# An attention and FFN block with adaptive layer norm: attention stage through the list scheduler, x1 of two blocks turned on VectorE

## The chip, the cores and the metric

One core of a Trainium2 chip runs the whole kernel. Its engines work side by side, each through its own list of instructions in order: TensorE (PE; its weight loads are listed as PEld), VectorE (DVE), ScalarE (ACT), GpSimd (POOL) and SyncE (SP). POOL and SP also issue most of the DMA transfers, so that an issue stands in their list behind what came before it. The metric is the device time of one execution, in microseconds (us). Smaller is better.

## The reference

A block with modulated layer norms: linear attention with a residual, then dense, Mish, dense with a residual. S is 2048 rows, D is 512, F is 1792, and there are 32 heads of 16.

```python
mod = (silu(c) @ w_mod).reshape(1, 6, 1, 512)
sa, ca, ga, sb, cb, gb = (mod[:, i] for i in range(6))
h = layernorm(x) * (1 + ca) + sa
q, k, v = split_heads(h @ wqkv)
phi = lambda t: where(t > 0, t + 1, exp(t)) + 1e-6
pq, pk = phi(q), phi(k)
kv = einsum("bhsd,bhse->bhde", pk, v)
z = pk.sum(over s)
o = (pq @ kv) / (pq . z + 1e-6)
x1 = x + ga * (merge_heads(o) @ wo)
h = layernorm(x1) * (1 + cb) + sb
out = x1 + gb * (mish(h @ w1 + b1) @ w2)
```

## The kernel before

**Data.** The 2048 rows are four blocks of 512 (b = 0 to 3), each of four row tiles of 128 (t). Features lie in four chunks of 128 (g, j or k). A product in full precision is three float32r matmuls, of the upper and lower halves of its operands (hi x hi, lo x hi, hi x lo). A *split* makes these halves: ACT rounds to the upper (name ending in h), VectorE subtracts to get the lower (ending in l).

**First part** (to line 940): layer norm, k = phi(...) of all rows, and the sums that stand for kv and z. z_unit (435) multiplies the summed pk (tile ku) by ones in plain float32, so that each partition has all of z. bcast_row (537) turns four columns of the modulation tile mc into a row with a TensorE transpose and an ACT copy, stores the row to DRAM and loads it back to all partitions; it serves ga (for wo) and gb (for the second residual).

**Attention stage** (943 to 1162). This code is written in the order in which its instructions stand. `tick` runs the generators that `spawn` has put in a list, one step of each, after each product. q of blocks 0 and 1 comes out of a seven-product scheme (q_sevens, 492), q of blocks 2 and 3 from plain products (q_unit, 442). attend (943) makes the denominators of a block: 16 plain float32 matmuls for four chunks and row tiles (line 948), TINY and reciprocal on VectorE (952), a store of the 64 KB to DRAM (955), four loads that spread them to 128 partitions (959, tile rd), and q times rd on VectorE (967) with a split. kv_ps (1098) is the kv product, m_k is kv times wo, and o_unit (993) is one row tile of the attention's output: four chunks of three matmuls. o_post adds x to get x1 and stores that to the output in DRAM.

x1 is then normalised row by row (norm_first, norm_each), and the FFN needs it transposed, features on partitions. For blocks 0 and 1, transpose_f (1032) and tp_op (1870) do this on TensorE: four 128x128 transposes into one PSUM tile tp_n for each of four chunks, which ACT scales and shifts to hf_n. For blocks 2 and 3, norm_job (1788) stores the rows to a DRAM tile nd, squares_job (1809) loads them back in four strips of 32x32 squares (tile y_n), and turn_job (1818) transposes the squares on VectorE, after which ACT scales.

**FFN stage** (from 1163). It works on pairs of blocks (0 with 1, then 2 with 3) and on seven groups g of 256 hidden features, again with seven products in place of eight: pair gives the first dense layer (products A to G, of six matmuls each), unit the second (m1 to m7). Their operands are sums and differences of quarters: t1 to t4 of the transposed x1 (columns_job, 1830), s of w1 (rows_job), t of w2 (sums_job; sums_first, 818, for two groups that are made in the attention stage). A list scheduler sets the order: drive (1290) takes the next TensorE operation that can start by its own clocks, and beside it the *jobs*, generators of steps for the other engines. best_job (1225) picks, on the engine that can start earliest, the waiting step with the nearest due time. The due times and the durations assumed are the table T (27). What is emitted stands in the engines' lists in that order; the chip doesn't reorder it.

Of the kernel before, what the change touches and what calls it, by code (L numbers as in the profile page):

```python
# [13 lines left out]
P = 128  # L14
# [15 lines left out]
 'urgent': 2.8,  # L30
 'store_later': 10.8,
 'row_lead': 21.6,
 'columns': 94.0,
# [4 lines left out]
 'lead_r': 12,  # L38
 'sum_lead': 3,
 'row_0': 31.7,  # L40
 'row_step': 12.1,
 'blocks': 11.6,
 'blocks_early': 19.3,
 'out_due': 57.7,
 'out_at': 20.3,
 'early_due': 98.6,
 'early_at': -0.5,
 'norm_due': 60.2,
 'norm_at': 18.7,
# [5 lines left out]
 'mm': 0.2166,  # L55
 'slow': 1.06,
 'late': 0.596,
 'pool_issue': 1.099,
 'left_early': 17.4,
 'right_due': 0.3,  # L60
 'right_early': 14.3,
 'sum_due': 0.3,
 'sum_early': 19.5,
 'pace_a': 5.2,
 'pace_l': 3.5,
 'pair_l': 13.2,
 'seq_0': 'ABCD.E.FG',
 'seq_l': 'AB.CD.E.FG..',
 'copy_due': 12.9,
# [7 lines left out]
 'first': 2,  # L77
 'turn_late': [5.0, 2.0],
 'left_out': 10.0,
 'add': 2.8}  # L80

@with_exitstack
def block_kernel(ctx: ExitStack, tc: tile.TileContext, x, wqkv, wo, w1, b1t, w2, c, wmodt, out):
# [351 lines left out]
    def z_unit():  # L435

        u = ku.pop((0, 0))
        p = ps("h", "z")
        pe.matmul(p, ones, u, start=True, stop=True)
        act.activation(zbc, p, AF.Identity, bias=ztiny[:, 0:1])  # L440

    def q_unit(b, g):
        p = ps("h", f"pq_{b}_{g}")
        gs = slice(P * g, P * (g + 1))
        for k in range(4):
            mm3(p, [w[:, gs] for w in wq[k]], hT["x", b, k], k == 0, k == 3)
        pq[b, g] = sb(f"q_{b}_{g}")
        spawn(phi(p, f"q_{b}_{g}", pq[b, g]))

# [42 lines left out]
    def q_sevens(side):  # L492

        pa, pc, u1, u2, u3 = {}, {}, {}, {}, {}

        def result(b, g, p, u):
            if u is not None:
                c = sb(f"cq_{b}_{g}")
                dve.tensor_tensor(c, p, u, op=ALU.add)
                p = c  # L500
            pq[b, g] = sb(f"q_{b}_{g}")
            spawn(phi(p, f"q_{b}_{g}", pq[b, g], 0 if u is None else 1 + (b == 0)))

        def copy(p, name):
            u = sb(name)
            act.activation(u, p, AF.Copy)
            return u

        for o in range(2):
            pa[o] = q_product(o, "a11", "b11", "h")  # L510
            u1[o] = copy(pa[o], f"qu1_{o}")
        side(0)
        for o in range(2):
            p = q_product(o, "a12", "b21", ("h", "tp")[o])
            result(0, o, p, u1[o])
            q_product(o, "s2", "t2", onto=pa[o])
            u2[o] = copy(pa[o], f"qu2_{o}")
            side(1 + o)
        for o in range(2):
            q_product(o, "s3", "t3", onto=pa[o])  # L520
            u3[o] = copy(pa[o], f"qu3_{o}")
# [1527 lines left out]
```

## Time and profile before

| | |
|---|---|
| median of 3 runs | 477.7 us (477.52 to 477.88) |
| span of the profiled execution | 475.7 us |
| TensorE's last matmul ends at | 471.3 us |
| attention stage after the first part, roughly | 103 to 197 us |
| first product of the FFN (p_a) | 196.85 us |

The span is that of one execution under the hardware profiler, from the first instruction to the last; the runs' times are the device's and hold 2.0 us more. In the timeline's rows, start and duration are followed by engine, line, operation, output and inputs. Matmuls are pipelined, so that a record of 0.39 us reaches into the next: the pace is read from start to start. In rows of groups, the number behind the bar is busy time and mean, then the idle time ahead and who ended it.

### The profile page before, as it was taken

How to read it: one execution, taken by the hardware profiler on the slowest of the kernel's cores; microseconds unless marked ns; L12 is line 12 of the kernel's file. 1: busy time of each engine (PE TensorE's matmuls, PEld its weight loads, DVE VectorE, ACT ScalarE, POOL GpSimd, SP SyncE). 2: the span in 40 equal slices, each digit the busy share in tenths (PEclk: the TensorE clock that was granted, in tenths of full speed). 3: DMA queues.
4: the chain of work that ended last, by engine and by line, in shares of the span. 5: the costliest groups of instructions: out<-in, count | busy, mean ns of one | idle time of the engine just before them, and what ended most of it. 6: DMA issues, size and time to landing. Idle time of an engine off the chain costs nothing.

```text
span 475.7 us, 7248 instructions
## 1 busy us (share of the span) xinstructions
PE 468.3 (98%) x2292; PEld 385.0 (81%) x2292; DVE 419.8 (88%) x816; ACT 325.1 (68%) x593; POOL 150.6 (32%) x220
## 2 busy tenths in 40 slices
PE   8999999999999999999999999999999999999996
PEld 6788888878877888888788888888888887788886
DVE  6989989898999998998998999989875767999984
ACT  6776777866835988769979898576466657546330
POOL 4684331100022422214433130522131325607340
PEclk9999999999999999999999999999999999999999
DMA  8998599434888486339899451983352469999977
GB/s 301 400 357 225 159 192 280 128 106 136 289 227 246 148 261 230 119 126 320 223 318 314 168 162 59 206 275 122 104 156 67 116 196 234 240 319 184 261 113 132
DMA packets 80480, 97.76 MB, mean 206 GB/s; under 512 B 29521, under 2 KB 53081, under 8 KB 80442
## 3 DMA queue, kind: packets, MB, share of 16 engines
q1 hardware_dynamic: 54376, 57.82, 39.3%
q0 software_dynamic: 22752, 38.43, 32.8%
q10 hardware_dynamic: 3314, 1.05, 1.1%
q8 instruction: 18, 0.29, 0.3%
q14 instruction: 20, 0.16, 0.1%
HBM read 69.22 MB, written 31.99 MB: 213 GB/s over the span
## 4 chain that ended last, share of the span: by engine, by line
PE 93%; DVE 3%; issue 1%; DMA 1%; ACT 1%; POOL 0%; ACTq 0%; DVEq 0%
PE p_a L1567 20%; PE pa L1652 12%; PE p_s L1567 8%; PE pc L1652 5%; PE pb L1652 4%; PE pd L1652 4%; PE o L142 3%; PE o L144 3%; PE o L143 3%; PE pq_a L488 3%; PE gacc L144 2%; PE pk L144 2%; PE gacc L142 2%; PE pk L142 2%; PE gacc L143 2%; PE pk L143 2%
## 5 line engine op out<-in xcount | busy, mean ns | idle before, releaser
L1526 POOL DMA_DIRECT2D wt_m<-w2t x32 | 28.0, 1109 | 56.0 <-PE p_a L1567 13.4
L1582 ACT ACTIVATE u<-p_a 128x512 f32<-128x512 f32 x42 | 25.0, 596 | 30.3 <-PE p_a L1567 29.7
L1591 ACT ACTIVATE u_a<-c_a,b1c 128x512 f32<-128x512 f32 x42 | 30.2, 719 | 14.9 <-DVE c_a L1588 12.9
L1717 POOL DMA_DIRECT2D out_dram<-turned x20 | 23.3, 1727 | 35.9 <-DVE turned L1705 25.0
L1588 DVE TENSOR_TENSOR c_a<-p_s,u 128x512 f32<-128x512 f32 x28 | 19.3, 689 | 15.7 <-PE p_s L1567 8.2
L1541 DVE TENSOR_TENSOR u_a<-u_a,u_a 128x512 f32<-128x512 f32 x28 | 18.6, 683 | 0.0
L984 POOL DMA_DIRECT2D out_dram<-r x16 | 9.0, 562 | 26.2 <-DVE r L988 13.6
L278 POOL TENSOR_TENSOR rs_n<-rs_n,half 128x1 f32<-128x1 f32 x16 | 10.8, 676 | 19.6 <-DVE rs_n L304 10.0
L1526 POOL DMA_DIRECT2D wt_m<-w2d x13 | 12.8, 1228 | 10.4 <-DVE c_a L1588 5.0
L371 ACT ACTIVATE e_k<-pk 128x512 f32<-128x512 f32 x15 | 8.9, 591 | 10.5 <-PE pk L144 10.4
L955 POOL DMA_DIRECT2D rden_d<-rden x2 | 1.4, 721 | 44.9 <-DVE rden L953 44.9
L1588 DVE TENSOR_TENSOR c_a<-p_a,u 128x512 f32<-128x512 f32 x14 | 9.6, 688 | 4.4 <-PE p_a L1567 1.7
L1683 ACT ACTIVATE U<-pa,mc 128x512 f32<-128x512 f32 x10 | 6.9, 685 | 9.4 <-PE pa L1652 9.3
L374 DVE SCALAR_TENSOR_TENSOR ku<-e_k,relu_k 128x512 f32<-128x512 f32 x15 | 10.7, 714 | 2.8 <-ACT relu_k L372 2.6
L278 POOL TENSOR_TENSOR rs_x<-rs_x,half 128x1 f32<-128x1 f32 (+1 forms) x10 | 7.9, 792 | 16.0 <-DVE rs_x L273 14.6
L1619 ACT ACTIVATE u_a<-p_a,b1c 128x512 f32<-128x512 f32 x14 | 9.6, 686 | 4.4 <-PE p_a L1567 4.3
L1368 POOL DMA_DIRECT2D w1p<-w1d x13 | 9.9, 765 | 8.0 <-PE p_a L1567 3.5
L967 DVE SCALAR_TENSOR_TENSOR q<-q,rd 128x512 f32<-128x512 f32 x16 | 10.5, 686 | 1.5 <-DMA rd<-rden_d 1.5
L374 DVE SCALAR_TENSOR_TENSOR q<-e_q,relu_q 128x512 f32<-128x512 f32 x16 | 10.6, 686 | 0.3 <-ACT relu_q L372 0.3
L254 DVE SCALAR_TENSOR_TENSOR wm<-wm,sc_row 128x512 f32<-128x512 f32 x16 | 10.6, 680 | 0.0
L1344 ACT ACTIVATE l_m_0h<-u_a 128x512 fp32r<-128x512 f32 x12 | 7.5, 623 | 4.3 <-DVE u_a L1541 4.3
L1350 DVE TENSOR_TENSOR l_m_1l<-u_a,l_m_1h 128x512 fp32r<-128x512 f32 x12 | 8.2, 685 | 2.0 <-ACT l_m_1h L1344 2.0
(1446 smaller groups left out, 1877.2 us busy)
## 6 DMA issues: line engine op xcount, KB each, us to landing
wt_m<-w2t POOLq DMA_DIRECT2D x32, 256.0 KB, 4.2
wt_m<-w2t SPq DMA_DIRECT2D x22, 256.0 KB
r<-in_x_dram SPq DMA_DIRECT2D x16, 256.0 KB
out_dram<-r POOLq DMA_DIRECT2D x16, 256.0 KB, 3.7
x<-in_x_dram SPq DMA_DIRECT2D x15, 256.0 KB
wt_m<-w2d SPq DMA_DIRECT2D x15, 256.0 KB
w1d<-in_w_dram SPq DMA_DIRECT2D x4, 896.0 KB
w1p<-w1d SPq DMA_DIRECT2D x13, 256.0 KB
```

What stands on the lines that cost most here:

```text
L142: pe.matmul(o, st[0], mv[0], start=start, stop=False)
L143: pe.matmul(o, st[0], mv[1], start=False, stop=False)
L144: pe.matmul(o, st[1], mv[0], start=False, stop=stop)
L278: pool.tensor_tensor(y, y, half[:, lo:hi], op=ALU.pow)
L374: dve.scalar_tensor_tensor(dst, e, 1.0, r, op0=ALU.min, op1=ALU.add)
L1526: q.dma_start(f32(v), (w2d if src == "w2d" else w2t)[g][:, :, part, :])
L1567: pe.matmul(p, st, mv, start=onto is None and c == 0 and i == 0, stop=c == 1 and i == 2, skip_group_check=onto is not None)
L1582: act.activation(t["u", n], t["pa"], AF.Copy)
L1588: dve.tensor_tensor(t[key], t[p], t["u", n], op=ALU.add)
L1591: act.activation(u, t[key], AF.Mish, bias=b1c[:, f:f + 1])
L1652: pe.matmul(o, st[:, cs], mv, start=not onto and n == 0 and k == 0, stop=n == G - 1 and k == 2, skip_group_check=onto)
L1717: q.dma_start(rows_, sq, accum_op=ALU.add)
```

## The change

**The attention stage is emitted by the list scheduler.** tick first runs until nothing of the first part is left. A new attention_stream yields the stage's TensorE operations, and its other work becomes jobs with due times in T; drive then goes on into the FFN without a break, and the due times of the FFN are counted from B, its start. VectorE's and ACT's clocks begin at T['behind'].

**Transposes.** Blocks 0 and 1 take the way of blocks 2 and 3: rows normalised with sums from ACT, stored to nd, loaded as y_n, transposed on VectorE, scaled on ACT. tp_n is gone.

**z** is two float32r products, of ones with the upper and the lower half of ku. **Denominators** of blocks 0 and 1, and of 2 and 3, are made together in one PSUM tile, with TINY added on ACT. **The gate rows** ga and gb are stored to DRAM from the columns, transposed by the DMA's addresses in elements of 4 bytes, and loaded back. **w2's sums** of two groups move from the attention stage to the FFN (T['first'] from 2 to 0), as do the gate columns 20 to 23 of the modulation (due at T['gate_due']). The other numbers of T are set anew.

```diff
- 'first': 2,
+ 'first': 0,
+ 'behind': 3.5,
...
+ 'gate_due': 160.0,
...
     def bcast_row(cols, name):
         yield
-        yield
-        p = ps("tp", f"{name}_ps")[0:4, 0:P]
-        pe.transpose(p, mc[:, cols:cols + 4], ident)
-        row = cst.tile([4, P], F32, tag="row", name=f"{name}_row", bufs=1)
-        act.activation(row, p, AF.Copy)
         d = drp.tile([4, P], F32, name=f"{name}_d")
-        pool.dma_start(d, row)
+        pool.dma_start(d.rearrange("k p -> p k"), mc[:, cols:cols + 4])
...
-        u = ku.pop((0, 0))
-        p = ps("h", "z")
-        pe.matmul(p, ones, u, start=True, stop=True)
...
+    def z_op(due):
+        def do():
+            p = ps("tp", "z")
+            for i in range(2):
+                pe.matmul(p, ones_r, zh_["z"][i], start=i == 0, stop=i == 1)
...
+    while running or fresh or idle_work:
         tick()
...
+        if b < 2:
+            yield a_(lambda: st.__setitem__(0, act_sums("n", b, t, v)), 1400, needs=x1)
+            yield d_(lambda: dve.tensor_scalar(rs["n", b][:, t:t + 1], st[0][:, 1:2], 1.0 / D, EPS, op0=ALU.mult,
+                                               op1=ALU.add), 4)
+            yield step_(POOL, 0.7, lambda: ln_rstd("n", b, t, t + 1))
+            yield d_(lambda: sums_shift("n", b, t, st[0]), 4)
...
+            yield a_(apply_, 750)
+            yield dma_(lambda q: to_dram("n", b, t, st[1], q), [("n", b, t)])
+            return
...
+    def den_op(bs, due):
+        def do():
+            p = ps("tp", f"den_{bs[0]}")
+            for n, b in enumerate(bs):
+                for g in range(4):
+                    for t in range(4):
+                        pe.matmul(p[32 * t:32 * (t + 1), P * n:P * (n + 1)], hmask[:, g, :],
+                                  pq[b, g][:, P * t:P * (t + 1)], start=g == 0, stop=g == 3)
...
+    def attention_stream():
...
+        yield from sevens()
+        yield kv_op(T['m_at'] - 3)
+        yield q_op(2, 0, T['den23'])
+        yield den_op((0, 1), (T['den01'] + 2, T['den01'] + 6))
+        for g in 1, 2, 3:
+            yield q_op(2, g, T['den23'])
+        for k in range(4):
+            yield m_op(k, T['m_at'] + 4)
+        for g in range(4):
+            yield q_op(3, g, T['den23'])
+        yield o_op(0, 0, now[0] + 3)
+        yield den_op((2, 3), (T['den23'] + 4, T['den23'] + 12))
...
+        for b, t in [(b, t) for b in range(3) for t in range(4)][1:]:
+            yield o_op(b, t, now[0] + 3)
...
-        yield tp_op(1, 1, "h")
-        yield o_op(0)
-        yield tp_op(1, 3, "h")
-        yield o_op(1)
+        yield from attention_stream()
+        ffn.append(True)
+        B = clock[PE] + 4 * 12 * MM
+        yield o_op(3, 0, B + 3)
+        yield o_op(3, 1, B + 6)
```

What this does to the engines' lists is shown at three places. A name's last number only counts tiles.

**TensorE, end of block 1's outputs, before.** o_3 is the last row tile of block 1; behind it stand the transposes of chunks 0 and 2 of block 0, then block 2's first row tile:

```order
L143 MATMUL o_3_2255<-m_3l,qs_3h 128x512
L144 MATMUL o_3_2255<-m_3h,qs_3l 128x512
L1035 MATMUL tp_n_0_2290<-ident,n_0_2055 128x128
L1035 MATMUL tp_n_0_2290<-ident,n_1_2095 128x128
L1035 MATMUL tp_n_0_2290<-ident,n_2_2135 128x128
L1035 MATMUL tp_n_0_2290<-ident,n_3_2171 128x128
L1035 MATMUL tp_n_2_2297<-ident,n_0_2055 128x128
L1035 MATMUL tp_n_2_2297<-ident,n_1_2095 128x128
L1035 MATMUL tp_n_2_2297<-ident,n_2_2135 128x128
L1035 MATMUL tp_n_2_2297<-ident,n_3_2171 128x128
L142 MATMUL o_0_2304<-m_0h,qs_0h 128x512
L143 MATMUL o_0_2304<-m_0l,qs_0h 128x512
```

After, behind block 2 and two row tiles of block 3 (o_1 here), the first product of the FFN follows at once, here with its first six matmuls:

```order
L162 MATMUL o_1_2377<-m_2h,qs_2l 128x512
L160 MATMUL o_1_2377<-m_3h,qs_3h 128x512
L161 MATMUL o_1_2377<-m_3l,qs_3h 128x512
L162 MATMUL o_1_2377<-m_3h,qs_3l 128x512
L1185 MATMUL p_a_0_2407<-b_0_0h,a_0h 128x512
L1185 MATMUL p_a_0_2407<-b_0_0l,a_0h 128x512
L1185 MATMUL p_a_0_2407<-b_0_0h,a_0l 128x512
L1185 MATMUL p_a_0_2407<-b_0_1h,a_0h 128x512
```

All 32 transposes of the stage are gone from this list; the o products and the products A and B of the FFN keep their order.

**POOL, around the FFN's start, before.** The x1 rows of block 2 (up to r_3) and of block 3 are stored (out_dram<-r), then w2's rows of the next group are loaded:

```order
L984 DMA out_dram<-r_0_1482 128x512
L984 DMA out_dram<-r_1_1524 128x512
L984 DMA out_dram<-r_2_1552 128x512
L984 DMA out_dram<-r_3_1572 128x512
L984 DMA out_dram<-r_0_1898 128x512
L984 DMA out_dram<-r_1_1920 128x512
L1442 DMA w2r_0_2577<-in_w_dram 128x512
L1442 DMA w2r_1_2585<-in_w_dram 128x512
```

After, the strips of the normalised rows (y_n from nd, both for blocks 0 and 1) are loaded among these stores:

```order
L1447 DMA y_n_2250<-nd_2035 32x16x128
L337 DMA nd_2244<-n_1_2252 128x512
L1447 DMA y_n_2250<-nd_2035 32x16x128 x2
L296 TENSOR_TENSOR rs_n_2150<-rs_n_2150,half 128x1
L779 DMA out_dram<-r_1_1742 128x512
L779 DMA out_dram<-r_2_1759 128x512
L1447 DMA y_n_2363<-nd_2244 32x16x128
L779 DMA out_dram<-r_3_1786 128x512
L1447 DMA y_n_2363<-nd_2244 32x16x128
```

The last strip of block 1 (y_n_2363) has moved in behind out_dram<-r_3_1786, the store of block 2's last x1 rows.

**VectorE, around the FFN's start, before.** The splits of block 0's and 1's transposed x1 (b) and the residual adds (r<-o) lead to the differences t of both:

```order
L156 TENSOR_TENSOR b_0_3l<-hf_n_3_2377,b_0_3h 128x512
L988 TENSOR_TENSOR r_3_1572<-o_3_2422,r_3_1572 128x512
L156 TENSOR_TENSOR b_1_2l<-hf_n_2_2420,b_1_2h 128x512
L1350 TENSOR_TENSOR b_1_1l<-hf_n_1_2463,b_1_1h 128x512
L1839 TENSOR_TENSOR t_0_t_2469<-hf_n_0_2384,hf_n_0_2295 128x512
L1863 TENSOR_TENSOR r_0_1898<-o_0_2450,r_0_1898 128x512
L1498 TENSOR_TENSOR t_0_2492<-w2r_0_2131 128x256
L1839 TENSOR_TENSOR t_1_t_2496<-hf_n_1_2463,hf_n_1_2338 128x512
L1498 TENSOR_TENSOR t_0_2492<-w2r_1_2132,t_0_2492 128x256
```

After, this place begins with the last splits of the scaled q (qs) and has the transposes of block 0; block 1's follow eleven rows later:

```order
L967 TENSOR_TENSOR qs_3l<-q_3_1917,qs_3h 128x512
L1495 TENSOR_TENSOR r_2_1759<-o_2_2299,r_2_1759 128x512
L1454 STREAM_TRANSPOSE hf_n_0_2340<-y_n_2250 128x512
L1454 STREAM_TRANSPOSE hf_n_1_2342<-y_n_2250 128x512
L1454 STREAM_TRANSPOSE hf_n_2_2345<-y_n_2250 128x512
L1454 STREAM_TRANSPOSE hf_n_3_2361<-y_n_2250 128x512
L1495 TENSOR_TENSOR r_3_1786<-o_3_2325,r_3_1786 128x512
L967 TENSOR_TENSOR b_0_0l<-hf_n_0_2340,b_0_0h 128x512
L967 TENSOR_TENSOR b_0_1l<-hf_n_1_2342,b_0_1h 128x512
L1495 TENSOR_TENSOR r_0_1871<-o_0_2347,r_0_1871 128x512
L1115 TENSOR_TENSOR t_0_2396<-w2r_0_1921 128x256
```

The residual add of r_3_1786, which makes the rows of block 2 that POOL's store waits for, stands behind the four transposes.

716 lines of the change are left out of this document (299 added, 417 removed).

## The prediction

> **What bounds the kernel now.** First the page: the busy shares and the chain that ended last.
>
> ```profile
> span 475.7 us, 7248 instructions
> ...
> PE 468.3 (98%) x2292; PEld 385.0 (81%) x2292; DVE 419.8 (88%) x816; ACT 325.1 (68%) x593; POOL 150.6 (32%) x220
> ...
> PE 93%; DVE 3%; issue 1%; DMA 1%; ACT 1%; POOL 0%; ACTq 0%; DVEq 0%
> ```
>
> TensorE is busy for 98% of the span and is 93% of the chain, so a microsecond taken from its stream is a microsecond of the kernel, as long as its operands still come in time. The windows by stage, chosen as the rest of the attention stage, the start of the FFN stage and its rest, say where they might not. Columns: length, then busy time of PE, PEld, DVE, ACT and POOL, the granted TensorE clock, the DMA share and GB/s.
>
> ```profile
> 103.00:197.00 94.00, 93.92 (x589) 75.90 (x588) 87.82 (x188) 70.12 (x134) 19.62 (x33) 1.00 0.66 205
> 197.00:310.00 113.00, 112.98 (x498) 92.85 (x497) 105.07 (x211) 94.58 (x177) 38.28 (x59) 1.00 0.72 207
> ```
>
> TensorE stands still for 0.1 us in both together. VectorE has 94.00 - 87.82 = 6.2 us left in the first and 113.00 - 105.07 = 7.9 us in the second: it is nearly a second bound. Sums are made against the span, 475.7; the median of the runs, 477.7, is 2.0 longer, and I carry these 2.0 unchanged. The granted clock is 1.00 in both windows and no part of the change lowers TensorE's share, so I leave it there.
>
> **Transposes off TensorE.** The PE rows at the end of the attention stage (start, duration), and a group of the tile tp_n (shortest, median and longest record in ns):
>
> ```profile
> 174.03 0.39 PE L142 MATMUL o<-m_0h,qs_0h 128*128 128x512 f32 x1
> ...
> 176.75 1.04 PE L1035 MATMUL tp_n<-ident,n 128*128 128x128 f32 x8
> ...
> 196.85 0.39 PE L1567 MATMUL p_a<-b_0h,a_0h 128*128 128x512 f32 x1
> ```
>
> ```profile
> L1035 PE MATMUL tp_n<-ident,n x24: 270/272/273, 176.8 to 187.6; 128*128 128x128 f32 x24
> ```
>
> One o product is 12 matmuls and takes 176.75 - 174.03 = 2.72 us, 0.227 each from start to start (a record's 0.39 overlaps the next). From 176.75 to 196.85 there are six o products, 6 x 2.72 = 16.32, and 32 transposes, these 24 and the 8 of L1875 (the change takes out all of both lines): 20.10 - 16.32 = **3.8 us**, all of which goes. That is 0.12 for each transpose, less than half of its record of 0.272, since they overlap.
>
> The Trainium skill, page "TensorE: Matmul & The Clock Gate", section "Part 4: PE-mode transpose", gives about 275 ns for a 128x128 transpose in one kernel's context; by it 8.8 us would go instead of 3.8. The record agrees, at 0.272 us, the distance between starts doesn't.
>
> **z in two float32r products.**
>
> ```profile
> 102.85 1.02 PE L439 MATMUL z<-ku,ones 128*128 128x512 f32 x2
> 103.30 0.80 PE L488 MATMUL pq_a<-hT_x_0h,wq_0h 128*128 128x512 f32 x1
> 103.94 0.40 PE L488 MATMUL pq_a<-hT_x_0l,wq_0h 128*128 128x512 f32 x1
> ```
>
> z and one ordinary matmul take 103.94 - 102.85 = 1.09; less 0.23 for the ordinary one z costs 0.86. Two float32r matmuls take 0.45: **0.4** goes. The split of ku is one more ACT and one more VectorE pass, beside the products q that now stand ahead of z.
>
> **The gate rows.**
>
> ```profile
> 86.39 0.27 PE L542 MATMUL ga_ps<-ident,mc 128*4 128x128 f32 x1
> ...
> 86.96 0.40 PE L144 MATMUL pk<-wk_0h,hT_x_0l 128*128 128x512 f32 x1
> ```
>
> Two ordinary starts lie between, so the transpose costs 0.57 - 0.45 = 0.12; two of them **0.2**. In their place stands a DMA of 512 elements of 4 bytes. No row shows such a store; by the transfers quoted below it lands after 3.2 to 10.5 us. VectorE needs ga only to scale wo for the m products, behind all products q of blocks 0 and 1, some 35 us later, and gb not before the FFN's second half. Both ends are covered: nothing, and as much as the delay beyond 35 us if the elements went one by one far slower than any row here.
>
> **Denominators in pairs.**
>
> ```profile
> 152.30 0.39 PE L144 MATMUL o<-m_3h,qs_3l 128*128 128x512 f32 x1
> 152.62 1.08 PE L948 MATMUL den<-q,hmask 128*32 128x128 f32 x32
> 153.63 0.50 PE L142 MATMUL o<-m_0h,qs_0h 128*128 128x512 f32 x1
> 153.97 0.40 PE L143 MATMUL o<-m_0l,qs_0h 128*128 128x512 f32 x1
> ```
>
> From 152.30 to 153.97 are 1.67 us; less two ordinary starts a den costs 1.22, while its own 32 matmuls run 1.01 to the next start. 0.2 is changing over into and out of plain float32. The 128 small matmuls stay, but they stand in three places instead of four (den 0 stood beside kv before): **0.2**. The sum is 3.8 + 0.4 + 0.2 + 0.2 = **4.6 us** off TensorE.
>
> **What x1 by DRAM asks in return.** The DMA issues (KB each, median us to landing), the transposes of blocks 2 and 3, which go this way already, and two VectorE rows back to back:
>
> ```profile
> rd<-rden_d POOLq DMA_DIRECT2D x8, 256.0 KB, 6.2
> ...
> nd<-r POOLq DMA_DIRECT2D x6, 256.0 KB, 3.2
> ...
> rq<-out_dram POOLq DMA_DIRECT2D x4, 256.0 KB, 10.5
> ...
> y_n<-nd POOLq DMA_DIRECT2D x1, 256.0 KB, 6.6
> ...
> rden_d<-rden POOLq DMA_DIRECT2D x2, 64.0 KB, 4.7
> ```
>
> ```profile
> L1822 DVE STREAM_TRANSPOSE hf_n<-y_n x8: 698/704/705, 248.6 to 273.1; 128x512 f32<-128x512 f32 x8
> ```
>
> ```profile
> 186.60 0.69 DVE L988 TENSOR_TENSOR r<-o,r 128x512 f32<-128x512 f32 x1
> 187.20 0.68 DVE L156 TENSOR_TENSOR qs_0l<-q,qs_0h 128x512 fp32r<-128x512 f32 x1
> ```
>
> VectorE's pitch is 0.60 (187.20 - 186.60) for a record of 0.69, and so about 0.61 for a transpose's 0.70. The eight new transposes are 8 x 0.61 = 4.9 us of VectorE, which in the attention stage more than leaves (below). What counts is the date. With 4.6 us gone, the FFN's first product starts at 196.85 - 4.6 = 192.2. Counting o products of 2.72 back from there (six of blocks 2 and 3, four of block 1), block 1's last o ends at 175.9 and block 0's at 165.0; counting forward (four half products A, B of 1.36, then two o), the product C of pair 0 starts at 203.1 and D at 204.5.
>
> ```profile
> L287 ACT ACTIVATE n<-r,nb_n,rs_n x8: 801/804/816, 160.8 to 183.2; 128x512 f32<-128x512 f32 x8
> ```
>
> ```profile
> L278 POOL TENSOR_TENSOR rs_n<-rs_n,half 128x1 f32<-128x1 f32 x16 | 10.8, 676 | 19.6 <-DVE rs_n L304 10.0
> ```
>
> Block 0: its last residual add stands on VectorE behind a scaling that waits for rd of block 2. Three o products before 165.0, at 156.8, den 2 and 3 end; with 1.2 for add and reciprocal, 4.7 for the store, 0.6 for issuing and 6.2 for the load that is 169.5. Two ACT passes for the sums and one to apply (0.80 each), the power on POOL (0.68) and small steps between them bring 173; nd's store 3.2 and POOL's queue lead to a last load issued between 177 and 180, which lands at 183.6 to 186.6 with y_n's 6.6; four transposes, ACT's scale and the split end at 190.4 at the latest. **Needed at 192.2: 2 us to spare.**
>
> Block 1: the last y_n load stands on POOL behind the x1 store of block 2's last row tile, and that store waits for a VectorE add behind the four transposes of block 0 (its o product ends before that, at 192.2 - 2 x 2.72 = 186.8): 183.6 to 186.6, 4 x 0.61, 0.6 for the add and 0.6 for issuing, so 187.3 to 190.3, and with 6.6 a landing at 193.9 to 196.9. C needs nine VectorE instructions after that (5.5 us): 199.4 to 202.4, in time for 203.1. The second half of D needs sixteen (16 x 0.61 = 9.7): 203.6 to 206.6, against 204.5 + 0.7. So **0 to 1.4 us of waiting, and from there on each us of delay is a us**; below nothing it can't go, as TensorE has no other work to take there. I take 0.3, since the middle of the landings, 195.4, is just in time.
>
> Denominators 0 and 1 together: between them and the first o stand seven q products and four m products, 7 x 2.72 + 4 x 0.68 = 21.8. The chain is ACT's add and the reciprocal 1.2, the store 4.7, four issues of 0.6, the landing 6.2, scale and split 2.0: 16.5. Denominators 2 and 3: seven o products stand between, 19.0, against the same 16.5. Both are covered, the second by 2.5 us, which is also all that a wait may grow to.
>
> VectorE in the FFN's start: T['first'] moves the w2 sums of two groups behind 197, and the gate columns go there too.
>
> ```profile
> L254 DVE SCALAR_TENSOR_TENSOR wm<-wm,sc_row 128x512 f32<-128x512 f32 x12 | 7.9, 680 | 0.0
> ...
> L829 DVE TENSOR_TENSOR t<-w2p,t 128x256 f32<-128x256 f32 x4 | 1.7, 422 | 0.1
> ```
>
> Eight half-width passes (pitch 0.33 of a record of 0.42), four splits at 0.60 and four gate columns at 0.68 are 7.8 us. That is what leaves the attention stage, and it is **all of the 7.9 us** free in 197 to 310. The order shows little slack there, 1.5 to 3 us for the first Mish results, so the cost lies between 0 and 3 us; below nothing is excluded, as no work leaves that stage. I take 0.3, because TensorE stands still there for 0.02 us today and these instructions have late due times.
>
> The Trainium skill, page "VectorE: DVE Perf Modes", section "Rules for kernel authors", says to transpose 128x128 on TensorE where a PSUM destination will do, as VectorE's transpose works in 32x32 blocks; that speaks against the change, and by it the 3.8 would stay and the sum be 476.9. The trace bears out its price (0.704 on VectorE for four, against 0.47 on TensorE), but here TensorE is the engine without idle time, so I don't follow it.
>
> **Sum:** 475.7 - 4.6 + 0.6 = 471.7 of span, and 2.0: **473.7 us**.
>
> **The rivals.** (1) The waits don't come: 473.1, within the forecast's range; and where some matmuls that start late now, hidden in the overlap of the records, come on time as well, 1 to 2 us less, 471.3 to 472.3. (2) Each transpose held TensorE for its record: 32 x 0.272 = 8.7 in place of 3.8, and 475.7 - 9.5 + 0.6 + 2.0 = 468.8; the starts quoted speak against it. (3) VectorE is the bound at the FFN's start: 7.8 us moved into 7.9, and where a split is late TensorE stands 1.5 to 3 us: 475.0 to 476.7. For it speaks the window's 93%; against it that nothing waits there today. (4) The y_n loads land like rq's row: 10.5 - 6.6 = 3.9 more, on top of 0 to 1.4: TensorE gives back 4 to 5, the time is 477.1 to 478.4 and can't be told from no change. (5) **Slower:** the round trip by DRAM. If block 0's rows are stored late too (5 us instead of 3.2), which shifts all that stands behind them, and the loads land like rq, D waits 1.4 + 3.9 + 1.8 = 7.1 and the time is 473.1 + 7.1 = 480.2. It decides where these delays pass 5.6 us (478.65 - 473.1). For it speaks a DMA share of 0.66 to 0.72 with POOL's queue in order; against it that y_n's and nd's own rows are the same transfers in the same load. That the change doesn't do what it says is no case of its own: the order shows the transposes gone, and only the dates are open, which are (3) to (5).
>
> **How the numbers follow.** Runs of this kernel can tell about 0.2% from no change, 0.96 us: "same" is 476.75 to 478.65. The forecast with its own range, 472.3 to 475.0, gets 0.49; (1) 0.08; (2) 0.02; (3) with up to 476.75, 0.18; (4) and other waits that end within the bound 0.11; (5) 0.12. Faster: 0.49 + 0.08 + 0.02 + 0.18 = 0.77. The range leaves out (2), the lowest of (1), the upper part of (4) and (5), some 0.2 together: 471.5 to 477.9, which takes in both ends of the wait for D, those of the FFN's start and most of rq's landing.
>
> **What would show it.** Right: no transposes on PE before the first p_a, 32 fewer rows; the first p_a near 192; y_n's last landing before 197; z's rows 0.23 apart; TensorE's busy share still 98%. Wrong: idle time of PE ended by b or t splits (L967 of the changed kernel) near 192 or 205, by the first c_a or l_m splits between 205 and 230, or by qs near 150 and 176. The forecast fails if the span's gain doesn't stand at the first p_a (then the products' pace changed), or if it stands there and is gone by 230 (then VectorE took it).

## The result, and the profile after

The changed kernel takes 496.4 us (median of four runs, 495.3 to 497.6) against 477.6 in the same session: a ratio of 1.039 with an interval of 1.037 to 1.042. The forecast was 473.7, with a range up to 477.9. It went the other way, by 18.8 us.

The page after, busy shares and the chain that ended last:

```profile
span 493.6 us, 7264 instructions
...
PE 471.1 (95%) x2258; PEld 384.1 (78%) x2258; DVE 419.8 (85%) x816; ACT 329.7 (67%) x604; POOL 165.5 (34%) x244
...
PE 66%; DMA 14%; DVE 7%; ACT 6%; issue 4%; POOL 1%; ACTq 0%; SPq 0%; DVEq 0%; POOLq 0%
```

TensorE's share of the chain fell from 93% to 66%, and DMA has 14% where it had 1%. VectorE's busy time is unchanged at 419.8. So no engine became the bound; TensorE now waits in many places, and the chain behind these waits runs mostly through transfers (14%), VectorE (7%) and ACT (6%). The same two stages by windows, split at the new start of the FFN (columns as before: length, PE, PEld, DVE, ACT, POOL, granted clock, DMA share, GB/s):

```profile
103.00:201.40 98.40, 91.48 (x553) 73.14 (x551) 73.88 (x156) 64.79 (x131) 28.64 (x46) 0.98 0.64 195
201.40:320.00 118.60, 109.01 (x458) 86.77 (x459) 105.68 (x214) 96.94 (x180) 34.13 (x56) 0.97 0.76 210
```

TensorE stands still for 98.40 - 91.48 = 6.9 us in the first and 9.6 in the second, where it stood 0.1 in both, and the granted clock is 0.98 and 0.97 instead of 1.00. Its longest waits (total, times, longest):

```profile
PE p_a L1185 <- ACT u L1200: 8.3, 4, 5.5
PE den L1680 <- DVE q L1585: 2.4, 2, 1.4
PE o L160 <- ACT qs_3h L961: 1.9, 1, 1.9
PE p_a L1185 <- ACT b_0h L961: 1.7, 2, 1.4
```

Only the last is the wait for x1's round trip, on which the prediction spent its main price. These are idle times. Counted as the excess of a start over the pace (gaps above 0.25 us, from 103 on) the waits sum to 19.3 us, before to 1.2. TensorE's last matmul starts at 489.06 instead of 471.03: 18.0 later = 18.1 more waiting, less 4.6 of work, and a remainder of 4.5. Some 3.5 of it, an estimate from the starts, are matmuls that start further apart in the stretches of low clock (0.50 to 0.74 in 268 to 276, 0.61 in 160 to 164); the rest isn't placed.

**The longest wait.** POOL stores the gate columns and loads the row back (start, duration, then the idle time before in brackets):

```profile
251.88 0.77 POOL L1779 DMA_DIRECT2D gb_d<-mc  x1 [0.21 <-issue]
267.72 0.54 POOL L1783 DMA_DIRECT2D gb_bc<-gb_d  x1 [15.07 <-DMA w2t<-t_0h]
```

The load waits for its store, and POOL, which works in order, stands 15.07 us. (The releaser named is a sums' store that ended last by the profile; the load reads what the gate store wrote, and in a later kernel below the same row names that store.) In the list of issues (median us to landing), the 15.6 us of this store of 2 KB is longer than every median of a transfer of 256 KB, two of which stand here beside the two stores:

```profile
y_n<-nd POOLq DMA_DIRECT2D x11, 256.0 KB, 7.4
...
nd<-n SPq DMA_DIRECT2D x7, 256.0 KB, 5.7
...
ga_d<-mc POOLq DMA_DIRECT2D x1, 2.0 KB, 10.0
gb_d<-mc POOLq DMA_DIRECT2D x1, 2.0 KB, 15.6
```

Meanwhile ACT waits for a transfer of another queue, in front of its work for the FFN:

```profile
260.48 0.72 ACT L1209 ACTIVATE u_a<-c_a,b1c 128x512 f32<-128x512 f32 x1
267.27 0.63 ACT L1071 ACTIVATE b<-w2r 128x512 fp32r<-128x512 f32 x1 [6.08 <-DMA nd<-r]
```

and the windows of 2 us show what follows:

```profile
262.00:264.00 2.00, 2.00 (x10) 1.65 (x10) 0.45 (x2) 0.00 (x0) 0.00 (x0) 1.00 0.95 55
264.00:266.00 2.00, 1.39 (x7) 0.81 (x5) 0.00 (x0) 0.00 (x0) 0.00 (x0) 1.00 0.88 61
266.00:268.00 2.00, 0.00 (x0) 0.00 (x0) 0.00 (x0) 0.72 (x2) 0.28 (x1) 1.00 0.99 221
268.00:270.00 2.00, 0.00 (x0) 0.00 (x0) 1.54 (x3) 1.97 (x4) 1.93 (x4) 0.74 1.16 302
270.00:272.00 2.00, 1.06 (x3) 0.87 (x4) 2.00 (x5) 2.00 (x4) 2.00 (x4) 0.50 0.94 140
272.00:274.00 2.00, 2.00 (x6) 1.61 (x5) 2.00 (x5) 1.43 (x4) 0.91 (x2) 0.50 0.98 314
```

Read the last two columns first: at a DMA share of 0.95 only 55 GB/s move. All compute engines run dry, TensorE last. When it starts again at 270.94, the clock is 0.50 and matmuls start 0.43 us apart (272.39, 272.81) instead of 0.23.

### The profile page after: what moved, and what is told of

It reads as the page before. It is cut to its first block, busy times and chain, and to the rows that moved or that the text cites. A ratio compares the mean times of both kernels' runs of the same rounds, so it can differ in the third digit from the quotient of the medians.

```text
span 493.6 us, 7264 instructions
## 1 busy us (share of the span) xinstructions
PE 471.1 (95%) x2258; PEld 384.1 (78%) x2258; DVE 419.8 (85%) x816; ACT 329.7 (67%) x604; POOL 165.5 (34%) x244
## 4 chain that ended last, share of the span: by engine, by line
PE 66%; DMA 14%; DVE 7%; ACT 6%; issue 4%; POOL 1%; ACTq 0%; SPq 0%; DVEq 0%; POOLq 0%
PE p_a L1185 11%; PE pa L1270 10%; DMA rd<-rden_d 6%; PE pc L1270 6%; PE p_s L1185 5%; PE pd L1270 4%; DMA w2t<-t_0h 3%; PE pq_a L491 3%; DMA y_n<-nd 3%; PE pb L1270 2%; PE gacc L162 2%; PE gacc L161 2%; PE pk L162 2%; PE pk L161 2%; PE gacc L160 2%
## 5 line engine op out<-in xcount | busy, mean ns | idle before, releaser
L1335 POOL DMA_DIRECT2D out_dram<-turned x20 | 22.0, 1722 | 33.1 <-DVE turned L1323 18.2
L1705 DVE SCALAR_TENSOR_TENSOR q<-q,rd 128x512 f32<-128x512 f32 x16 | 10.9, 687 | 14.2 <-DMA rd<-rden_d 9.6
L1457 ACT ACTIVATE hf_n<-hf_n,mc 128x512 f32<-128x512 f32 x16 | 12.6, 806 | 6.1 <-DVE hf_n L1454 5.9
L389 ACT ACTIVATE e_k<-pk 128x512 f32<-128x512 f32 x15 | 8.9, 595 | 10.9 <-PE pk L162 10.2
L1454 DVE STREAM_TRANSPOSE hf_n<-y_n 128x512 f32<-128x512 f32 x16 | 10.6, 692 | 5.7 <-DMA y_n<-nd 4.1
L779 POOL DMA_DIRECT2D out_dram<-r x10 | 5.7, 572 | 24.2 <-DVE r L1495 14.2
L1585 DVE SCALAR_TENSOR_TENSOR q<-e_q,relu_q 128x512 f32<-128x512 f32 x16 | 10.8, 685 | 3.2 <-ACT relu_q L1581 3.1
L1757 POOL DMA_DIRECT2D r<-in_x_dram x11 | 6.0, 559 | 22.0 <-PE pq_s L491 7.5
L392 DVE SCALAR_TENSOR_TENSOR ku<-e_k,relu_k 128x512 f32<-128x512 f32 x15 | 10.7, 713 | 2.8 <-ACT relu_k L390 2.7
L1495 DVE TENSOR_TENSOR r<-o,r 128x512 f32<-128x512 f32 x16 | 10.8, 682 | 0.5 <-PE o L162 0.5
L967 DVE TENSOR_TENSOR l_m_6l<-u_a,l_m_6h 128x512 fp32r<-128x512 f32 x12 | 8.1, 680 | 3.3 <-ACT l_m_6h L961 3.3
L272 DVE SCALAR_TENSOR_TENSOR wm<-wm,sc_row 128x512 f32<-128x512 f32 x16 | 10.6, 674 | 0.0
```

The lines of the kernel that those rows point to most:

```text
L1335: q.dma_start(rows_, sq, accum_op=ALU.add)
```

## The experiments

Each ran with the kernel before beside it (477.5 to 477.9), and its ratio is to that. Differences are in us, to the kernel that was edited; for the changed kernel that is the 496.4 of its own session.

**Single parts taken back in the changed kernel.** First the gate store: gb's columns stored as they stand, 128 pieces of 16 bytes, so that the gate row has another order and the output with it.

```diff
-            s[0] = drp.tile([4, P], F32, name="gb_d")
-            q.dma_start(s[0].rearrange("k p -> p k"), mc[:, 20:24])
+            s[0] = drp.tile([P, 4], F32, name="gb_d")
+            q.dma_start(s[0], mc[:, 20:24])
```

> The changed kernel with one transfer altered and every engine's order kept: the gate columns gb are stored as they stand, 128 runs of 16 bytes, instead of transposed in 512 elements of 4 bytes (the gate row is then in another order, so the second residual is scaled by other numbers). Theory A, the store of single elements holds up the transfers behind it: the store's landing falls from 15.6 us to under 6, ACT's 6.1 us wait for w2's rows at 261 to 267 goes, and with it TensorE's 5.6 us wait at 265 and the half clock of the 5 us behind it (2.5 us more), perhaps the 2.0 us at 285: 484 to 489 us. Rival, the transfers of that moment (w2t, w1p, y_n, w2r together) are too many whatever the store: 495 to 497 us and the wait stays.

492.98, ratio 1.032 [1.030, 1.034]: 3.4 less. ACT and POOL at the same place:

```profile
261.89 0.63 ACT L1071 ACTIVATE b<-w2r 128x512 fp32r<-128x512 f32 x1 [0.17 <-DMA nd<-r]
```

```profile
262.35 0.54 POOL L1783 DMA_DIRECT2D gb_bc<-gb_d  x1 [9.43 <-DMA w2t<-t_0h]
```

ACT's 6.08 are gone. The transfer that it waited for is, by the profile, a store of normalised rows on SP's queue (nd<-r). In the changed kernel it was issued at 251.00 and ACT was released at 267.27, 16.3 us later; here 251.50 and 261.89, 10.4 us. Only the gate store was altered, so its elements had slowed a transfer of another queue. POOL is still held 9.4 us, by a store that was expected to land in under 6, and another wait of 3.9 appears at 278. To part the hold from the elements, the load back was made a job of its own, due 40 us later (SP issues it), with the elements kept:

```diff
-        yield dma_(back)
+        add_job(iter([dma_(back)]), now[0] + 60, now[0] + 40)
```

> The changed kernel with the gate row's load back moved 40 us later and to SP's queue, so that POOL isn't held by its wait of 15 us; the store in 4-byte elements stays where it was, and TensorE's order is unchanged. If the hold on POOL is what costs (the loads of y_n, the stores of w2d and the powers stand behind it): the time falls by 3 to 6 us, to 490 to 493, and TensorE's wait at 265 goes. If the element store itself crowds out the other transfers: ACT still waits for w2's rows until 267, and the time stays at 495 to 497.

494.5, ratio 1.0345 [1.031, 1.038]: 1.9 less, with an interval that overlaps those of both neighbours. TensorE's wait of 5.7 at 265 became 3.1 + 1.7 + 0.6. But POOL wasn't free: with the gate row's load gone it stood at its next load, of rows whose store is in flight beside the elements:

```profile
264.13 1.95 POOL L1447 DMA_DIRECT2D y_n<-nd  x3 [10.02 <-DMA nd<-r]
```

So this edit moved the hold and didn't take it away. How much is hold and how much elements isn't settled.

Denominators one by one, the first before kv, the others spread between q and o:

```diff
+        yield den_op((0,), (T['den01'] + 2,))
         yield kv_op(T['m_at'] - 3)
         yield q_op(2, 0, T['den23'])
-        yield den_op((0, 1), (T['den01'] + 2, T['den01'] + 6))
+        yield den_op((1,), (T['den01'] + 6,))
...
+        yield den_op((2,), (T['den23'] + 4,))
         yield o_op(0, 0, now[0] + 3)
-        yield den_op((2, 3), (T['den23'] + 4, T['den23'] + 12))
+        yield o_op(0, 1, now[0] + 3)
+        yield den_op((3,), (T['den23'] + 12,))
```

> The changed kernel with the four denominators made one by one (block 0 ahead of kv, block 1 behind q of block 2's first chunk, block 2 ahead of the first o, block 3 behind the second o) instead of in pairs; the scheduler sets the rest of the order anew. Theory B, pairs make eight loads of rd come at once behind a store that waits in both DMA queues, and the second pair waits for q of block 3: the waits of TensorE between 127 and 187 us (7 us with the slow clock behind them) shrink to 0 to 3 us, and the time is 489 to 493 us. Rival, the queues are late for another reason (the scheduler's clocks run ahead of the chip): waits of the same sum at other places, 495 to 498 us.

489.59, ratio 1.024 [1.021, 1.026]: **6.8 less**, the largest single gain. What the pair did stands in the changed kernel's TensorE rows; both groups wait for q of block 3, whose products stand only one o product ahead:

```profile
157.29 0.42 PE L1680 MATMUL den<-q,hmask 128*32 128x128 f32 x8 [1.01 <-DVE q L1585]
...
159.09 0.42 PE L1680 MATMUL den<-q,hmask 128*32 128x128 f32 x8 [1.38 <-DVE q L1585]
```

Why q is late stands in VectorE's list: the two steps of q came behind a scaling that waited for rd of blocks 0 and 1.

```profile
155.94 0.69 DVE L1705 SCALAR_TENSOR_TENSOR q<-q,rd 128x512 f32<-128x512 f32 x1 [2.73 <-DMA rd<-rden_d]
156.55 0.68 DVE L1585 SCALAR_TENSOR_TENSOR q<-e_q,relu_q 128x512 f32<-128x512 f32 x1
```

The first pair's matmuls end at 129.1, so this scaling starts 26.8 us after them. And in the tile rd, whose users sat idle until its loads landed (us, times), changed kernel:

```profile
  DMA rd<-rden_d: 9.6, 5
```

kernel before:

```profile
  DMA rd<-rden_d: 1.5, 2
```

With the denominators apart it is 3.4, and TensorE's waits ahead of the FFN fall to a single one of 1.2 us.

Both of these together:

> The changed kernel with both earlier edits: denominators one by one, and the gate columns gb stored as they stand in runs of 16 bytes (the gate row is then in another order). If the two costs are separate they add: 496.4 - 6.8 - 3.4 = 486 us. If the store of gb only cost what it did because of the late attention stage (one cost seen twice), no better than 489.

488.35, ratio 1.022 [1.018, 1.027]: only 1.2 below the denominators alone. By the median the two costs overlap; a plain sum, 486, lies just outside the interval (486.4 to 490.6).

The w2 sums of two groups back in the attention stage ('first': 2):

> The changed kernel with T['first'] at 2 again: the w2 sums of two groups (four loads, eight half-width differences, eight stores of 256 KB) go back out of the stretch from 240 to 290 us. Theory D, that stretch is bound by the DMA engines (share 1.0 for 40 us) and the sums moved in are what overfills it: the waits of TensorE behind 260 us (8 us with the slow clock 11) fall to under 4 and the time to 486 to 491. Rival, the scheduler orders the rest as badly (what is late comes from before): 494 to 500.

498.5, ratio 1.042 [1.038, 1.047]: no gain. In the changed kernel as it stands this part isn't what costs.

x1 of blocks 0 and 1 back on TensorE, within the scheduler's order (transposes between the o products, ACT takes them from PSUM):

```diff
-            yield dma_(lambda q: to_dram("n", b, t, st[1], q), [("n", b, t)])
...
-                add_job(turn_job(b, j), (T['turn0'] if b == 0 else T['turn1']) + 0.5 * j)
+        turns = {8: [(0, 0), (0, 2)], 9: [(0, 1)], 10: [(0, 3), (1, 0)], 11: [(1, 2)]}
         for b, t in [(b, t) for b in range(3) for t in range(4)][1:]:
+            for i, j in turns.get(4 * b + t, ()):
+                yield tp_op(i, j)
             yield o_op(b, t, now[0] + 3)
```

> The changed kernel with x1 of blocks 0 and 1 turned on TensorE as before (32 transposes, no round trip by DRAM); the scheduler sets the rest anew. Theory C, the round trip costs about 3.3 us of waiting at the FFN's start and the transposes 3.8 us of TensorE: 496 to 498 us, that is no gain either way. Rival, the round trip's 16 transfers and the transposes on VectorE also make the waits in the FFN or those for rd: 488 to 493 us.

507.02, ratio 1.0605 [1.056, 1.065]: 10.6 **more**, which no theory expected. Transposes wait for rows that are normalised late (2.9), and products of the FFN for u and c_a (4.0 and 5.2 at 260 to 272). The due times are still those of the way by DRAM, so I don't read this as the price of TensorE's transposes.

**Single parts put into the kernel before.** ga and gb by DMA in elements of 4 bytes:

```diff
-        p = ps("tp", f"{name}_ps")[0:4, 0:P]
-        pe.transpose(p, mc[:, cols:cols + 4], ident)
-        row = cst.tile([4, P], F32, tag="row", name=f"{name}_row", bufs=1)
-        act.activation(row, p, AF.Copy)
         d = drp.tile([4, P], F32, name=f"{name}_d")
-        pool.dma_start(d, row)
+        pool.dma_start(d.rearrange("k p -> p k"), mc[:, cols:cols + 4])
```

> The kernel before with this one part of the change: ga and gb go to DRAM transposed in elements of 4 bytes, without the two TensorE transposes. Theory A (the store holds up others for 10 to 16 us): gb's store stands at 144 us among the denominators' loads, so these land some 5 to 10 us late and TensorE waits 2 to 8 us: 479 to 486 us. Rival, as I forecast (nothing but two transposes gone): 477.3 to 477.7 us.

481.79, ratio 1.009 [1.007, 1.011]: **4.1 more**. The stores land after 10.9 and 11.0 us, where the rows from TensorE took 1.6 and 5.1. POOL:

```profile
149.91 0.83 POOL L542 DMA_DIRECT2D gb_d<-mc  x1
161.49 0.56 POOL L544 DMA_DIRECT2D gb_bc<-gb_d  x1 [10.75 <-issue]
```

The powers of the layer norm stand behind on POOL; VectorE waits 2.75 for one, an o product 1.7 for its qs.

The w2 sums out of the attention stage ('first': 0):

> The kernel before with T['first'] at 0 alone: the w2 sums of two groups made in the FFN stage. Theory D as a cost of its own: the transfers of 230 to 260 us, where the share is 1.0 already, spread to 290 us and TensorE waits 2 to 6 us: 479 to 484. My forecast's term (VectorE fills up, 0.3 us, at most 3): 477.7 to 480.7, with TensorE's waits ended by VectorE, not by late loads.

481.48, ratio 1.007 [1.005, 1.010]: **3.6 more**, and not at the FFN's start but at 309 to 318, where TensorE stands 0.7 and 1.8 us for a split of VectorE, and at 410, where it stands 1.7 for a load of a w2 sum (wt_m). A VectorE row at the first place:

```profile
310.95 0.69 DVE L1588 TENSOR_TENSOR c_a<-p_s,u 128x512 f32<-128x512 f32 x1 [0.98 <-DMA w2t<-t_3h]
```

It waits for a buffer that the store of a w2 sum still reads; ACT waits 1.2 us there for another of these stores. The DMA share doesn't mark the place: it is 1.23 in 300 to 310, and 1.18 in the kernel before. TensorE also waits for such a load, at 410 to 422, in the gate run above (1.3 us) and in the three runs with x1 by DRAM below (0.8 to 1.6); in the kernel before it waits 0.1 there. So a part of each difference stands far from its edit, and why isn't shown.

z alone, two float32r products and the split that they need:

```diff
-        u = ku.pop((0, 0))
         p = ps("h", "z")
-        pe.matmul(p, ones, u, start=True, stop=True)
+        for i in range(2):
+            pe.matmul(p, ones_r, zh_["z"][i], start=i == 0, stop=i == 1)
```

> The kernel before with z in two float32r products alone. The forecast's term: 0.4 us less on TensorE, 477.3; nothing that these runs can tell from no change, but z's two rows stand 0.23 us apart and no wait of TensorE comes. Rival: the split of ku delays z and the q products behind it by 1 to 2 us: 478.5 to 479.5.

478.81, ratio 1.0018 [1.0005, 1.0032]: 1.1 more. In this place the second product waits 0.63 us for the lower half, which comes out of the split too late. In the changed kernel z's rows are 0.23 apart, as forecast.

x1 of both blocks by DRAM: rows stored with to_dram, the strips loaded by ACT's queue, four transposes on VectorE, no tp_op:

```diff
+    def strips(b):
+        yd["n", b] = big.tile([P, 4 * 512], F32, tag="Y", name=f"y_n_{b}", bufs=YS)
+        for c in range(4):
+            act.dma_start(*strip_squares(yd["n", b], nd["n", b], c))
+
+    def turns(b):
+        for j in range(4):
+            hf[b, j] = sb(f"hf_n_{b}_{j}")
+            dve.transpose(hf[b, j], chunk(yd["n", b], j))
...
-        ln_apply("n", 0, t, nat(xt["r", 0, t]), lin(v), act)
+        ln_apply("n", 0, t, xt["r", 0, t], v, act)
+        to_dram("n", 0, t, v)
```

> The kernel before with one part of the change: x1 of blocks 0 and 1 stored to DRAM after the norm, loaded as squares and turned on VectorE, the 32 transposes taken off TensorE, in the hand-written order (loads on ACT's queue, so that neither SP nor POOL waits). My forecast's main term: 3.8 us go, waits of 0 to 1.4 us at the FFN's start come: 474 to 476. Rival, the round trip is late as in the changed kernel (3.3 us of waits or more): 477 to 481.

491.74, ratio 1.028 [1.024, 1.031]: **13.9 more**. VectorE in this kernel:

```profile
195.86 0.69 DVE L967 SCALAR_TENSOR_TENSOR q<-q,rd 128x512 f32<-128x512 f32 x1 [1.02 <-DMA rd<-rden_d]
198.91 0.69 DVE L967 SCALAR_TENSOR_TENSOR q<-q,rd 128x512 f32<-128x512 f32 x1 [2.36 <-DMA rd<-rden_d]
199.52 0.68 DVE L988 TENSOR_TENSOR r<-o,r 128x512 f32<-128x512 f32 x1
200.12 2.48 DVE L1008 STREAM_TRANSPOSE hf_n<-y_n 128x512 f32<-128x512 f32 x4
202.52 0.65 DVE L156 TENSOR_TENSOR qs_2l<-q,qs_2h 128x512 fp32r<-128x512 f32 x1
```

The round trip is not what is late here, but block 3's rd: from the first issue of its loads to its last scaling are 16.7 us (182.21 to 198.91), in the kernel before 10.7 (178.80 to 189.54), and TensorE then waits for qs_2l. The DMA share is 0.96 and 1.02 in 170 to 180 and 180 to 190, where it was 0.65 and 0.76. That the added transfers delay rd by sharing the DMA engines is my reading of this; no run shows it alone. The transposes, which I put ahead of that split, are 2.5 us of it. So block 0 alone, its transposes behind the qs:

> The kernel before with x1 of block 0 alone turned by way of DRAM (16 transposes less on TensorE, 8 transfers of 256 KB more; VectorE's transposes stand behind the splits of q). If the price lies in the added transfers that make rd of block 3 late (16 of them cost 13.9 + 3.8 us in the run with both blocks), half of them cost less than half, as they end before rd of block 3 is issued: waits of 2 to 7 us against 1.9 us gained, 478 to 483. If it lay in the order of VectorE's queue: no wait for qs, 475.5 to 477.5.

489.33, ratio 1.023 [1.021, 1.025]: 11.6 more, against 478 to 483 expected. Half the transfers cost nearly all: waits for qs of 2.4 in sum, and the FFN's first product waits 1.1 and 4.6 for b, so that here the round trip itself is late. And both blocks with loads in runs of 2 KB to a partition (x1 then stands in another order, so the FFN computes something else):

```diff
-            act.dma_start(*strip_squares(yd["n", b], nd["n", b], c))
+            act.dma_start(yd["n", b][:, 512 * c:512 * (c + 1)], nd["n", b][P * c:P * (c + 1), :])
```

> The run with both blocks by way of DRAM, with one thing altered: the loads of the normalised rows fetch the same 256 KB in runs of 2 KB to 128 partitions instead of 512 bytes to 32 partitions (x1's FFN input is then in another order). Theory: short runs take more of the DMA engines' time per byte, so the loads squeeze rd: with long runs rd lands 3 to 8 us earlier and the time falls from 491.7 to 480 to 488. Rival: the bytes are what counts, or the stores ahead: 490 to 493.

487.79, ratio 1.020 [1.017, 1.0235]: 3.9 below the strips. The shape of the strips is a part; most stays, and the wait for qs_2l is there again (4.8).

**Several parts taken back in the changed kernel.** Denominators alone, transposes on TensorE, gb in 16 bytes:

> The changed kernel with three parts undone at once: denominators one by one, x1 of blocks 0 and 1 turned on TensorE, the gate columns gb stored as they stand (gate row in another order). What is left of the change is the scheduler's order of the attention stage, z, ga and T. If the parts are the cause: TensorE's waits behind 103 us fall to 2 to 6 us and the time to 477 to 483. If the scheduler's order itself is (its durations for transfers are too short, so loads stand too late): 488 to 500, with waits at the FFN's start and behind 250 us.

491.97, ratio 1.030 [1.028, 1.032]: 14.3 of loss stay, with POOL held again and VectorE behind it:

```profile
252.14 0.59 POOL L1783 DMA_DIRECT2D gb_bc<-gb_d  x1 [8.24 <-DMA gb_d<-mc]
```

```profile
253.89 0.55 DVE L307 TENSOR_SCALAR r<-r,mv_n,rs_n 128x512 f32<-128x512 f32 x1 [4.27 <-POOL rs_n L296]
```

The power rs_n stands behind the held load, and a p_s product waits 3.1 us for a c_a of VectorE there. Then the same with 'first': 2 and the load back 40 us later:

> The run with three parts undone (denominators one by one, x1 turned on TensorE, gate columns stored in 16-byte runs), and besides T['first'] at 2 and the gate row's load back 40 us later. Only the scheduler's order of the attention stage with its numbers, z, ga's store and the gate columns' place are left of the change. If the parts explain the loss: TensorE's waits behind 250 us fall from 8 to under 3 us and the time from 492.0 to 479 to 485. If it stays above 488, the loss is in the scheduler's order, whatever it is given.

486.95, ratio 1.020 [1.018, 1.022]; the waits left are 7.5 for the transposes' rows, which are normalised too late for them. And, as its pair, all of that but x1 by DRAM as in the change:

> As the run before in this call, but with x1 of blocks 0 and 1 by way of DRAM as in the change; so the difference of the two is that part in the scheduler's order. My forecast's term, 3.8 us off TensorE and about as much waiting: within 2 us of the other run. As in the kernel before (13.9 us lost): 8 us or more above it.

485.33, ratio 1.016 [1.014, 1.018], the lowest of the changed family and still 7.8 above the kernel before. It is within 2 us of its partner, as expected, but that says little, as the partner has 7.5 us of waits of its own. In all three pairs within the scheduler's order the way by DRAM is the faster (by 10.6, 3.6 and 1.6 us), each time with due times that were made for it. TensorE at the FFN's start:

```profile
192.59 0.39 PE L162 MATMUL o<-m_3h,qs_3l 128*128 128x512 f32 x1
196.58 0.50 PE L1185 MATMUL p_a<-b_0h,a_0h 128*128 128x512 f32 x1 [3.60 <-ACT b_0h L961]
```

SP, POOL and VectorE show why b of block 0 is late; the rows are its last store, its first and its last load, and the first transpose:

```profile
174.84 0.33 SPq L337 DMA_DIRECT2D nd<-n  x1
183.86 0.32 SPq L1447 DMA_DIRECT2D y_n<-nd  x1
```

```profile
185.62 0.70 POOL L1447 DMA_DIRECT2D y_n<-nd  x1
```

```profile
189.50 0.69 DVE L967 TENSOR_TENSOR t_3l<-t,t_3h 128x512 fp32r<-128x512 f32 x1
193.74 0.71 DVE L1454 STREAM_TRANSPOSE hf_n<-y_n 128x512 f32<-128x512 f32 x1 [3.55 <-DMA y_n<-nd]
```

With the other disturbances gone, this is the prediction's own case, and its dates can be compared. Its waits behind 103 sum to 12.0 us; 5.0 are p_a for b of block 0 and 3.7 the products C and D for the t of block 1.

## Why the prediction was wrong, point by point

The work came out as forecast. What failed are the terms for waiting, which the sum put at 0.6 us in all: the two transfer times of x1's round trip, what the pairs of denominators wait for and hold up, and what the gate store holds up. In the change TensorE's waiting grew by 18.1 us, and some 3.5 us of low clock came on top.

**The work: right.** "4.6 us off TensorE" holds: in the last kernel the last o ahead of the FFN starts its last matmul at 192.59 with a wait of 0.7 ahead of it (at 178.48), so the FFN could start at some 192.1; forecast 192.2. Nothing of the loss is in the work.

**"Needed at 192.2: 2 us to spare": wrong by sizes.** In the last kernel the rows of block 0 are normalised at 174.0 to 174.8 (173 forecast). From the last store's issue to the first strip's are 9.0 us (183.86 - 174.84), where nd's 3.2 was taken. The last load is issued at 185.6 (177 to 180 forecast) and VectorE starts at 193.7, 8.1 later, where y_n's 6.6 was taken; the landing was to be at 183.6 to 186.6. The 3.2 was the median of six stores from POOL's queue (2.3 to 6.2) and the 6.6 a single load; the list has no landing for SP's. The kernel before shows a slower case of its own, in block 3, whose last two rows were stored by SP and POOL:

```profile
239.55 0.32 SPq L319 DMA_DIRECT2D nd<-r  x1
```

```profile
250.91 0.92 SPq L1815 DMA_DIRECT2D y_n<-nd  x2
251.39 0.69 POOL L1815 DMA_DIRECT2D y_n<-nd  x1 [3.41 <-DMA nd<-r]
```

The strips came 11.4 us after SP's store was issued and 8.9 after POOL's (241.99), with POOL standing idle for it. So the prediction's point against rival 5, that block 3's transfers are "the same transfers in the same load", speaks for it instead. This is rival 5's mechanism, the only one on the right side, but it is worth 8.7 us of waiting (5.0 and 3.7), not the 7.1 that it was given, and in the change itself it is only part of the loss.

**"Both are covered, the second by 2.5 us": wrong.** The chain was priced, but not what the pair itself waits for: den of block 3 stands one o product behind the products that make its q (1.01 and 1.38 us of waiting). And the chain was too short: from the end of the first pair's matmuls to its last scaling are 26.8 us, where the terms up to the landing sum to 14.5, and behind that scaling, in order, stood VectorE's steps for that q. Idle time for rd is 9.6 us in all instead of 1.5. Undoing the pairs gives 6.8, where 0.2 had been booked as a gain.

**"VectorE needs ga only ... Both ends are covered: nothing": wrong.** The date of the gate row was priced, with a landing of 3.2 to 10.5 us; it was 10.0 and 15.6, and still in time. What costs is what the store holds up: POOL, in order, for 15.07 us behind a store of 2 KB, and the other queue's transfers. 4.1 us alone in the kernel before, 3.4 in the change.

**VectorE at the FFN's start, 0.3 taken of 0 to 3: wrong mechanism.** VectorE's work in the FFN window didn't fill it: 105.68 of 118.60. The same edit alone costs 3.6, outside the range of 0 to 3: a wait of 1.8 at 318 comes through buffers that late stores of w2's sums hold, and one of 1.7 at 410 is for a late load of a sum. In the change as it stands, undoing it alone brings nothing, which agrees with costs that hide behind one another.

**"The granted clock is 1.00 ... so I leave it there": wrong.** After the wait of some 6 us the clock is 0.50, and eleven matmuls start 0.43 us apart instead of 0.23, some 2.4 us more; after the waits before 160 it is some 1.5.

**The sum of it.** Along one path: 496.4, denominators apart 489.6, gb in 16 bytes 488.4, sums in the attention stage and the late load back 485.3. Another path would give other shares. Against the kernel before 7.8 us stay; in the profiled execution the last start is 8.8 later (479.85), which is 10.8 more waiting (12.0 against 1.2, 8.7 of it x1's) and some 1.6 of low clock, less 4.6 of work; 1.0 isn't placed. Two rivals were seen to be no cause: that VectorE is full, and that the transposes held TensorE for their record.

**Open.** How much of the 13.9 and 11.6 of x1 by DRAM in the kernel before is the transfers and how much the place that I gave its steps in VectorE's and ACT's lists; what TensorE's transposes would cost in the scheduler's order with due times made for them; the hold of POOL against the elements; and what the scheduler's order costs by itself: with x1 on TensorE and the other parts undone the kernel stays 9.5 above the kernel before, 7.5 of it waits for rows that are normalised late. Whether x1's remaining 8.7 us could be had back by earlier norms or another queue wasn't tried. No kernel here beat the one before.

## What to carry to other kernels

Price a new transfer not by its own landing alone but by what it shares: the queue that its wait holds up, and the DMA engines that all others need, since for an engine without slack a median over some transfers of one queue is no bound: look at the slowest, and at the transfers whose landing the list doesn't give. Here the trace before already had a release after 11.4 us where 3.2 was taken. Ask of every step that is moved, paired or scattered "what stands behind it in order", also when its result is needed much later. When several small losses sit on one loaded resource, they need neither add nor come back one by one, as the sums of w2 here: undo them together, and read the last wait.

## What the runs showed of the hardware

- A 2 KB store as 512 elements of 4 bytes landed after 10.0 to 15.6 us in the change, 10.9 and 11.0 in the kernel before with it, and the same bytes as four rows after 1.6 and 5.1. While the one of 15.6 us was under way, 38 to 61 GB/s moved in 260 to 266, at a DMA share of 0.75 to 0.95. In pieces of 16 bytes its load back still waited 9.4 us, but ACT's wait of 6.08 us for a transfer of the other queue was gone; from that transfer's issue to ACT's release were 16.3 us beside the elements and 10.4 beside the pieces of 16 bytes.
- The granted clock fell 3.6 us into TensorE's standstill of nearly 6 us (265.4 to 269.0) to 0.50, stayed there to 275.8, through the first matmuls, which started 0.43 us apart instead of 0.23, and was 1.00 again from 276. The waits of 1 to 1.4 us at 156 to 159 were followed by 0.61 in 160 to 164.
- In the kernel before, the loads that read two stores of normalised rows (256 KB each) were issued 11.4 and 8.9 us after these stores, while the median of six such stores was 3.2 us to landing (2.3 to 6.2).
